# Sigmoid attention and a SiLU layer on one core: bursts of three score tiles instead of two, the third in single PSUM banks

## The chip, the cores and the metric

The kernel runs on one core of one Trainium2 chip. The metric is device time in microseconds (us) of one execution, the median of several runs. Engines are named as in the profile: PE is TensorE's matmul queue, PEld its weight loads, DVE is VectorE, ACT is ScalarE, POOL is GpSimd, SP is SyncE, which here issues transposes and stores.

## The reference

Attention over 8 batches, 12 heads, 448 positions and 64 channels a head, with a sigmoid in place of the softmax, and behind it a dense layer, SiLU, and a second dense layer:

```python
scores = scale * np.matmul(q, k.transpose(0, 1, 3, 2)) - np.log(S)
attn = 1.0 / (1.0 + np.exp(-scores))
x = np.matmul(attn, v)                  # 8 x 12 x 448 x 64
x = x.transpose(0, 2, 1, 3).reshape(3584, 768)
h = x @ w_in                            # 768 -> 2048
g = h * (1.0 / (1.0 + np.exp(-h)))
out = g @ w_out                         # 2048 -> 768
```

Inputs and output are float32; the kernel computes with float16 operands and float32 sums.

## The kernel before

The 12 heads of a batch are worked on in three groups of four, so there are 24 groups (g) in all. A group's keys are cut into seven pieces (ch) of 64 positions. One piece of one group is a unit, or a tile of scores; there are 168, in the order of `units`, 21 to a batch.

**Scores** (`scores`, L168 to L186). Four 64x64 matmuls with 448 columns each fill a PSUM tile `psc` of two banks; they run side by side in the four quarters of TensorE. Then one activation on ACT (L184) reads both banks, takes the sigmoid with scale and with the bias tile `bias_s`, and writes `attnT` in float16. `psc` comes from the pool `ps_sc`, which has two such tiles and so four banks.

**Values** (`values`, L195 to L221). When the seven pieces of a group are there, seven rounds of four 64x64 matmuls add up in two banks `pav`; two DVE instructions (L219) copy them into `xT`.

**The dense layers** are a stream, written as a generator (`all_moe`). `h_unit` (L230 to L252) does one of 16 column blocks of the first layer for one batch: six 128x128 matmuls with 448 columns into a bank `ph`, a sigmoid on ACT (L248, `tsig`), a product on DVE (L249) into `gTr`. The second layer works on sets (`out_set`): a pair of row blocks is computed with seven products of half size in place of eight, each of eight matmuls with 384 columns into a bank `po` (`product`, L307), whose sums and differences DVE makes before (tiles `S1` to `S4`, from `gTr`) and after (L315, some banks with two readers). The first product of a set is copied by ACT (L322, `m`). The third product takes its weights from the first sum, `sg[2]` (tile `S3`), which DVE computes behind the last `gTr` of the batch.

`ph`, `po` and `pav` come from the pool `ps_1`, a ring of four single banks (tag `ps1`). The pool hands out the bank that was released longest ago in the program's order.

**The order** is written out by hand (`manual_schedule`): each engine does its instructions in the order of the program, and a wait holds whatever stands behind it on that engine. The last loop alternates a burst of scores with a piece of the stream. `stretch(ns)` adds ns to what is due, and takes steps of the stream, each with its planned time (189 ns an h matmul, 163 ns one of a product), until that much is done; it can stop inside an h unit or a product. `hold` keeps it going from the last h unit of a batch to the copy of the next set's first product. With each burst, `values_if_any` does the values of a group that is complete, and `rows_if_any` prepares one transpose: a copy on DVE (`kr` or `qr`, L163), a DMA transpose on SP, and behind q's the loads of k and q of a later group on POOL. `after_values` loads v. The piece of the stream behind a burst of two has a length by batch, `paces`, from 2,000 ns in batch 2 to 3,400 ns in batches 4 and 5.

Of the kernel before, what the change touches and what calls it, by code (L numbers as in the profile page):

```python
# [11 lines left out]
F32 = mybir.dt.float32  # L12
AF = mybir.ActivationFunctionType
# [4 lines left out]
def kernel(  # L18
# [9 lines left out]
    nc = tc.nc  # L28

    B, H, S, D = q.shape  # L30
    NT, DMODEL = out.shape
    DFF = moe_w_in.shape[1]
    P = 128
    HP = P // 2
    NCH = S // HP
    NPAIR = H // 2
    NQ = NPAIR // 2
    NT_B = NQ * NCH
# [7 lines left out]
    QKSCALE = 1.0 / math.sqrt(D)  # L46
# [7 lines left out]
    ps_sc = ctx.enter_context(tc.tile_pool(name="ps_sc", bufs=2, space=bass.MemoryType.PSUM))  # L54
    ps_1 = ctx.enter_context(tc.tile_pool(name="ps_1", bufs=4, space=bass.MemoryType.PSUM))
# [45 lines left out]
    bias_s = cpool.tile([P, 1], F32, tag="biass", name="bias_s")  # L101
# [65 lines left out]

    attnT = {}  # L168

    def scores(g, ch):  # L170
        attnT[g, ch] = p12.tile([P, 2, S], F16, tag="attnT", name="attnT")
        psc = ps_sc.tile([P, 2, 512], F32, tag="pssc", name="psc")
        for half in range(2):
            own = slice(half * HP, (half + 1) * HP)
            for j in range(2):
                rows = slice(j * D, (j + 1) * D)
                nc.tensor.matmul(  # L177
                    psc[own, j, :S],
                    qkT["k", g][rows, ch, own],
                    qkT["q", g][rows, :, own],  # L180
                    start=True,
                    stop=True,
                )
        nc.scalar.activation(  # L184
            attnT[g, ch], psc[:, :, :S], AF.Sigmoid, bias=bias_s, scale=QKSCALE
        )  # L186

    xT = {}
    ready = set()
# [4 lines left out]
    def values(g, end=NCH):  # L194
        b, iq = divmod(g, NQ)  # L195
        if b not in xT:
            assert b < 2 or b - 2 in h_done
            xT[b] = p2.tile([P, NPAIR, S], F16, tag="xT", name="xT")
        pav, done_rounds = part_of.pop(g, None) or (
            [ps_1.tile([P, 512], F32, tag="ps1", name="pav") for _ in range(2)],  # L200
            0,
        )
        for ch in range(done_rounds, end):
            at = attnT.pop((g, ch))
            for half in range(2):
                own = slice(half * HP, (half + 1) * HP)
                for j in range(2):
                    nc.tensor.matmul(  # L208
                        pav[half][j * D : (j + 1) * D, :S],
                        flat["v", g][own, j, ch, :],  # L210
                        at[own, j, :],
                        start=(ch == 0),
                        stop=(ch == NCH - 1),
                    )
        if end < NCH:
            part_of[g] = pav, end
            return
        for half in range(2):
            nc.vector.tensor_scalar_mul(xT[b][:, half * NQ + iq, :], pav[half][:, :S], SX)  # L219
        if iq == NQ - 1:  # L220
            ready.add(b)  # L221
# [177 lines left out]
    def stretch(ns):  # L399
        nonlocal done, due  # L400
        due += ns
        while done < due or hold:
            step_ns = next(stream, None)
            if step_ns is None:
                break
            done += step_ns
# [19 lines left out]
    units = [(g, ch) for g in range(NQB) for ch in range(NCH)]  # L426
    waiting = []
# [12 lines left out]
    def after_values(g):  # L440
        if g == 0:
            load("v", 3)
            load_w_in(2)
            load_w_in(3)
        elif g == 1:
            load("v", 4)
            load_w_out(0, 0)
            load_w_out(0, 1)
        elif g == 2:
            load("v", 5)  # L450
            load_w_out(1, 0)
            load_w_out(1, 1)
            load("kq", 6)
            load("kq", 7)
        elif g + 3 < NQB:
            load("v", g + 3)
        if g == 6:
            for to in (10, 11, 12):
                load("kq", to)
        if g == 5:  # L460
            load("kq", 9)
        if g >= 6 and g + 3 < NQB:
            later.extend(((g + 3, "k"), (g + 3, "q")))
# [3 lines left out]
    def rows_if_any():  # L467
        if later:
            g, name = later.pop(0)
            dma_transpose(g, name, nc.vector.tensor_copy)  # L470
            if name == "q" and g + 4 < NQB and g + 4 > 12:
                load("kq", g + 4)

    def values_if_any():
        if waiting:
            g = waiting.pop(0)
            values(g)
            after_values(g)
# [9 lines left out]
    def transposes(g, name):  # L488
        pe_transpose(g, ((name, 0, 4), (name, 4, NCH)))
        if name == "q":  # L490
            after_transpose(g)
# [35 lines left out]
    for n in range(NT_B + 3):  # L527
        scores(*units[n])
        for do, *what in behind.get(n, ()):
            do(*what)  # L530

    paces = {1: 1600, 2: 2000, 3: 2550, 4: 3400, 5: 3400, 6: 3000, 7: 3000}
    stretch(paces[1])
    for n in range(NT_B + 3, len(units), 2):
        burst = units[n : n + 2]
        if n == 2 * NT_B:
            values_if_any()
            stretch(21500)
        for u in burst:
            scores(*u)  # L540
        values_if_any()
        rows_if_any()
        for g, ch in burst:
            if ch == NCH - 1:
                waiting.append(g)
        if n in (24, 30):
            transposes(4 + (n - 24) // 6, "k")
        elif n in (26, 32):
            transposes(4 + (n - 26) // 6, "q")
        stretch(paces[1] if 1 not in ready else paces[n // NT_B])  # L550
    for g in waiting:
        values(g)
    for _ in stream:
# [31 lines left out]
```

## Time and profile before

| | us |
|---|---|
| median of 3 runs (382.05 to 382.88) | 382.63 |
| the profiled execution | 382.75 |
| its span, from the first to the last instruction | 381.0 |
| ACT, sigmoid of a tile of scores, mean of 168 | 1.016 |
| ACT, sigmoid of an h unit, mean of 128 | 0.545 |
| DVE, product of an h unit, mean of 128 | 0.623 |
| DVE, copy out of a values bank, mean of 48 | 0.619 |
| DVE, copy of the rows for a transpose | 0.61 |
| DVE, read of a product's bank | 0.55 |

The profiled execution's time is that of the profile's own run, 1.75 us of it outside the span. In the profile's groups, the number behind the bar is the busy time of the group, then the mean of one instruction in ns, then the idle time of its engine just before. The length of a matmul is that of its way through the array; matmuls overlap, and the distance between the starts of two neighbours is what one costs. In the timeline, instructions of one kind that follow each other are merged into one line with their number behind the x; the first number is the start, the second the time to the end of the last. Where a line says idle, it is the time that the engine waited ahead of it, with what ended the wait. A bank's wait is found in the start of a matmul behind its neighbour.

The granted TensorE clock is 1.00 throughout.

### The profile page before, as it was taken

To read this page: it belongs to the slowest core of one execution; us is meant where nothing else is said; L and a number is where in the kernel's file an instruction comes from. 1 tells how busy PE (TensorE), PEld (TensorE's weight loads), DVE (VectorE), ACT (ScalarE), POOL (GpSimd) and SP (SyncE) were. 2 spreads that over 40 slices of the span, in tenths; PEclk is the share of its full clock that TensorE was granted. 3 is DMA by queue.
4 is the path that set the end of the run, shared out by engine and by line. 5 is a ranking of instruction groups with operands and counts; after the bars stand their busy time and mean duration, and the time that the engine had idled before them with its cause. 6 is when DMAs were issued, how large, how long until landed. Compare 5 with 4: busy or idle time off the path is not lost.

```text
span 381.0 us, 7663 instructions
## 1 busy us (share of the span) xinstructions
PE 372.2 (98%) x3083; PEld 186.9 (49%) x3083; DVE 233.8 (61%) x415; ACT 240.0 (63%) x328; POOL 92.9 (24%) x158
## 2 busy tenths in 40 slices
PE   7999999999999999999999999999999999999995
PEld 2444445545554445444555444544455444555663
DVE  2446646996565666556767547735857446656773
ACT  4998886758777875778444686577774787044000
POOL 8855326202752323121311303101100000000000
PEclk9999999999999999999999999999999999999999
DMA  7999999974999936937939859535346300110233
GB/s 112 180 188 204 205 203 181 155 103 101 166 236 232 141 51 97 184 47 75 152 68 191 96 112 122 56 101 74 48 77 105 83 3 2 41 41 2 75 92 83
DMA packets 66403, 42.71 MB, mean 112 GB/s; under 512 B 37056, under 2 KB 62912, under 8 KB 66368
## 3 DMA queue, kind: packets, MB, share of 16 engines
q0 software_dynamic: 28032, 22.69, 42.7%
q1 hardware_dynamic: 38112, 19.31, 28.2%
q8 instruction: 24, 0.39, 0.4%
q10 hardware_dynamic: 224, 0.23, 0.2%
q14 instruction: 11, 0.09, 0.1%
HBM read 45.61 MB, written 11.01 MB: 149 GB/s over the span
## 4 chain that ended last, share of the span: by engine, by line
PE 80%; DMA 12%; DVE 2%; ACT 2%; POOL 1%; issue 1%; DVEq 0%
PE po L307 34%; PE ph L236 29%; PE psc L177 9%; PE pav L208 6%; DMA w_in_sb<-in_moe_w_in_dram 6%; DMA w_out_sb<-in_moe_w_out_dram 5%; DVE gTr L249 1%; DMA ks<-in_k_dram 1%; ACT attnT L184 1%; DMA vf<-in_v_dram 1%; DVE T L278 1%; POOL qf L78 1%; PE pw L135 1%; POOL kf L78 0%; ACT qr L138 0%
## 5 line engine op out<-in xcount | busy, mean ns | idle before, releaser
L184 ACT ACTIVATE attnT<-psc,bias_s 128x896 f16<-128x896 f32 x168 | 158.9, 1016 | 53.3 <-PE psc L177 53.2
L236 PE MATMUL ph<-xT,w_in_sb 128*128 128x448 f16 x768 | 153.2, 353 | 0.0
L249 DVE TENSOR_TENSOR gTr<-ph,tsig 128x448 f16<-128x448 f32 x128 | 78.1, 623 | 72.0 <-ACT tsig L248 71.4
L236 PEld LDWEIGHTS <-w_in_sb 128*128 128x128 f16 x768 | 71.9, 98 | 75.7 <-issue 12.9
L248 ACT ACTIVATE tsig<-ph 128x448 f16<-128x448 f32 x128 | 68.2, 545 | 47.8 <-PE ph L236 46.2
L78 POOL DMA_DIRECT2D vf<-in_v_dram x48 | 28.7, 613 | 140.7 <-PE pav L208 140.2
L307 PEld LDWEIGHTS <-S 128*128 128x128 f16 x448 | 42.3, 98 | 33.9 <-issue 6.8
L315 DVE SCALAR_TENSOR_TENSOR osb<-po,osb 128x384 f32<-128x384 f32 x70 | 37.7, 555 | 25.1 <-PE po L307 24.5
L177 PE MATMUL psc<-qT,kT 64*64 64x448 f16 x672 | 50.4, 362 | 2.5 <-ACT attnT L184 1.2
L219 DVE TENSOR_SCALAR xT<-pav 128x448 f16<-128x448 f32 x48 | 27.7, 619 | 30.3 <-PE pav L208 30.3
L307 PE MATMUL po<-T,S 128*128 128x384 f16 x224 | 40.6, 327 | 0.1
L307 PEld LDWEIGHTS <-gTr 128*128 128x128 f16 x304 | 28.7, 98 | 23.4 <-issue 5.2
L307 PE MATMUL po<-w_out_sb,S 128*128 128x384 f16 x224 | 39.9, 326 | 0.0
L208 PE MATMUL pav<-attnT,vf 64*64 64x448 f16 x672 | 37.9, 349 | 0.4 <-DVE gTr L249 0.4
L78 POOL DMA_DIRECT2D qf<-in_q_dram x48 | 28.9, 612 | 38.1 <-DVE qr L163 16.9
L307 PE MATMUL po<-w_out_sb,gTr 128*128 128x384 f16 x192 | 34.7, 327 | 0.0
L177 PEld LDWEIGHTS <-kT 64*64 64x64 f16 x672 | 15.0, 104 | 32.8 <-issue 30.9
L78 POOL DMA_DIRECT2D kf<-in_k_dram x48 | 28.9, 612 | 7.0 <-DVE kr L163 4.4
L208 PEld LDWEIGHTS <-vf 64*64 64x64 f16 x672 | 20.2, 107 | 12.4 <-issue 1.9
L315 DVE SCALAR_TENSOR_TENSOR osb<-po,m 128x384 f32<-128x384 f32 x42 | 23.2, 552 | 4.1 <-PE po L307 2.5
L322 ACT ACTIVATE m<-po 128x384 f32<-128x384 f32 x14 | 6.9, 491 | 23.7 <-PE po L307 23.7
L307 PE MATMUL po<-T,gTr 128*128 128x384 f16 x112 | 21.4, 326 | 0.0
(40 smaller groups left out, 131.0 us busy)
## 6 DMA issues: line engine op xcount, KB each, us to landing
out_dram<-osb SPq DMA_DIRECT2D x54, 192.0 KB, 2.9
qf<-in_q_dram POOLq DMA_DIRECT2D x48, 112.0 KB, 5.8
vf<-in_v_dram POOLq DMA_DIRECT2D x48, 112.0 KB, 4.8
kf<-in_k_dram POOLq DMA_DIRECT2D x46, 112.0 KB, 5.5
w_in_sb<-in_moe_w_in_dram POOLq DMA_DIRECT2D x4, 768.0 KB, 10.5
w_out_sb<-in_moe_w_out_dram POOLq DMA_DIRECT2D x4, 768.0 KB, 17.0
kT<-kr SPq DMA_TRANSPOSE x18, 5.6
qT<-qr SPq DMA_TRANSPOSE x18, 6.2
```

The source lines that it names most:

```text
L78: nc.gpsimd.dma_start(flat[name, g][half * HP : (half + 1) * HP, :, c0:c1].rearrange("p i c d -> p i (c d)"), source[name][b, h0 : h0 + 2] ...
L135: nc.tensor.matmul(pw, dummy[:, :P], dummy, start=True, stop=True)
L177: nc.tensor.matmul(psc[own, j, :S], qkT["k", g][rows, ch, own], qkT["q", g][rows, :, own], start=True, stop=True,)
L184: nc.scalar.activation(attnT[g, ch], psc[:, :, :S], AF.Sigmoid, bias=bias_s, scale=QKSCALE)
L208: nc.tensor.matmul(pav[half][j * D : (j + 1) * D, :S], flat["v", g][own, j, ch, :], at[own, j, :], start=(ch == 0), stop=(ch == NCH - 1),)
L219: nc.vector.tensor_scalar_mul(xT[b][:, half * NQ + iq, :], pav[half][:, :S], SX)
L236: nc.tensor.matmul(ph[:, :S], w_in_sb[:, cc, fc * P : (fc + 1) * P], xT[b][:, cc, :], start=(at == 0), stop=(at == NCC - 1),)
L248: nc.scalar.activation(tsig, ph[:, :S], AF.Sigmoid, bias=0.0, scale=ISX)
L249: nc.vector.tensor_mul(gTr[:, fc, (b % 2) * S : (b % 2) * S + S], ph[:, :S], tsig)
L307: nc.tensor.matmul(po[:, :NO2], a[:, fc, :], w[:, fc, :], start=(fc == 0), stop=(fc == NHC - 1))
L315: nc.vector.scalar_tensor_tensor(out=o, in0=po, scalar=sign, in1=x, op0=ALU.mult, op1=ALU.add)
L322: nc.scalar.activation(m1, po, AF.Copy, scale=ISX)
```

## The change

From batch 2 on, without batch 3, a burst has three tiles. It has two where a group waits for its values. The first of the three gets two single banks of the ring `ps_1`, and its sigmoid becomes two activations of 448 elements, one for each bank; the other two use the pool `ps_sc` as before. The piece of the stream behind a burst is as long per tile as before: `ns * tiles / 2`. What follows a burst (values, one transpose, the list of groups that wait) is done as before, once a burst. The part ahead of batch 2 keeps its order.

```diff
-    def scores(g, ch):
+    def scores(g, ch, banks=None):
         attnT[g, ch] = p12.tile([P, 2, S], F16, tag="attnT", name="attnT")
-        psc = ps_sc.tile([P, 2, 512], F32, tag="pssc", name="psc")
+        if banks is None:
+            psc = ps_sc.tile([P, 2, 512], F32, tag="pssc", name="psc")
+            banks = [psc[:, j] for j in range(2)]
+            parts = [(attnT[g, ch], psc[:, :, :S])]
+        else:
+            parts = [(attnT[g, ch][:, j], banks[j][:, :S]) for j in range(2)]
...
-                    psc[own, j, :S],
+                    banks[j][own, :S],
...
-        nc.scalar.activation(
-            attnT[g, ch], psc[:, :, :S], AF.Sigmoid, bias=bias_s, scale=QKSCALE
-        )
+        for to, psc in parts:
+            nc.scalar.activation(to, psc, AF.Sigmoid, bias=bias_s, scale=QKSCALE)
+
+    def single_banks():
+        return [ps_1.tile([P, 512], F32, tag="ps1", name="psc1") for _ in range(2)]
...
+    TILES = {2: 3, 3: 2, 4: 3, 5: 3, 6: 3, 7: 3}
     paces = {1: 1600, 2: 2000, 3: 2550, 4: 3400, 5: 3400, 6: 3000, 7: 3000}
-    stretch(paces[1])
-    for n in range(NT_B + 3, len(units), 2):
-        burst = units[n : n + 2]
-        if n == 2 * NT_B:
-            values_if_any()
-            stretch(21500)
-        for u in burst:
-            scores(*u)
+    def burst(n, tiles):
+
+        new = units[n : n + (tiles if not waiting else 2)]
+        for i, u in enumerate(new):
+            scores(*u, single_banks() if i == len(new) - 3 else None)
         values_if_any()
         rows_if_any()
-        for g, ch in burst:
-            if ch == NCH - 1:
-                waiting.append(g)
+        waiting.extend(g for g, ch in new if ch == NCH - 1)
+        return len(new)
+
+    stretch(paces[1])
+    for n in range(NT_B + 3, 2 * NT_B, 2):
+        burst(n, 2)
...
+    values_if_any()
+    stretch(21500)
+    n = 2 * NT_B
+    while n < len(units):
+        ns = paces[n // NT_B]
+        tiles = burst(n, TILES[n // NT_B])
+        n += tiles
+        stretch(ns * tiles / 2)
```

More of the change, by code (lines that the diff above doesn't have):

```diff
@@ L549 @@
             transposes(4 + (n - 26) // 6, "q")
-        stretch(paces[1] if 1 not in ready else paces[n // NT_B])
+        stretch(paces[1])
+    values_if_any()
[6 more added lines that the diff above has]
+        stretch(ns * tiles / 2)
     for g in waiting:
```

## Prediction

> **What bounds the kernel now.** I read the busy table first, then the waits, then the timeline of TensorE. The busy table:
>
> ```profile
> PE 372.2 (98%) x3083; PEld 186.9 (49%) x3083; DVE 233.8 (61%) x415; ACT 240.0 (63%) x328; POOL 92.9 (24%) x158
> ```
>
> PE works 98% of the span; every other engine has a third or more to spare. The waits of PE, from the view of who waited for whom:
>
> ```profile
> PE pw L135 <- DVE bias_s L422: 1.5, 1, 1.5
> PE psc L177 <- ACT attnT L184: 1.2, 4, 0.5
> PE psc L177 <- DVE qT L155: 0.5, 1, 0.5
> PE pav L208 <- DVE gTr L249: 0.4, 1, 0.4
> ```
>
> In 381 us the matmul queue waits 3.6 us. So what counts is the sum of TensorE's own work, anything that makes it wait is added whole, and neither DMA nor the 37% idle ScalarE can give anything by itself. Now PE's timeline in batch 4:
>
> ```profile
> 169.21 1.11 PE L236 MATMUL ph<-xT,w_in_sb 128*128 128x448 f16 x5
> 170.25 0.57 PE L177 MATMUL psc<-qT,kT 64*64 64x448 f16 x8
> 170.76 3.58 PE L236 MATMUL ph<-xT,w_in_sb 128*128 128x448 f16 x18
> 174.26 0.57 PE L177 MATMUL psc<-qT,kT 64*64 64x448 f16 x8
> ...
> 183.60 0.57 PE L177 MATMUL psc<-qT,kT 64*64 64x448 f16 x8
> ...
> 187.62 0.57 PE L177 MATMUL psc<-qT,kT 64*64 64x448 f16 x8
> ```
>
> Columns are start and length. Eighteen h matmuls and one burst of two tiles take 174.26 - 170.25 = 4.01. In the long run at the end 96 h matmuls take 18.16, 0.189 each, so 3.41 for 18. Tiles of scores inside a block follow at 0.189 (in the values at 209.29 seven rounds of the same 64x64 form take 1.43 to the next product at 210.72). 4.01 - 3.41 - 0.38 leaves 0.22 to 0.23 that a burst costs for going to 64x64 and back. Between products: 187.62 - 183.60 = 4.02, less 21 x 0.162 (runs of 20 and 21 differ by 0.162), less 0.38: 0.24. **A burst has an entry price of 0.23**, whatever its number of tiles.
>
> **The gain.** The order of the instructions is fixed by the program. The 126 tiles of scores of batches 2 to 7 stand in 63 bursts of two before and in 50 bursts after: 26 of three, 24 of two (batch 3, and each burst with values). 13 entries fall away: 13 x 0.233 = **3.03 us** off PE. The tiles themselves stay: 13 fewer bursts move 26 tiles into others, as third tile, at 0.187 to 0.189. The upper bound of a third tile is that of a tile alone, 0.31 (10.95 to 11.26). I take 0.189: it is the same form as the values' rounds, which keep 0.189 through seven rounds although each brings four weight loads. Nothing else that PE issues changes in number.
>
> **ScalarE.** 26 sigmoids of 896 become 52 of 448 that carry the bias tile. No such row exists. The nearest rows:
>
> ```profile
> L184 ACT ACTIVATE attnT<-psc,bias_s 128x896 f16<-128x896 f32 x168 | 158.9, 1016 | 53.3 <-PE psc L177 53.2
> L248 ACT ACTIVATE tsig<-ph 128x448 f16<-128x448 f32 x128 | 68.2, 545 | 47.8 <-PE ph L236 46.2 <-DVE T L278 0.6
> L322 ACT ACTIVATE m<-po 128x384 f32<-128x384 f32 x14 | 6.9, 491 | 23.7 <-PE po L307 23.7
> L138 ACT ACTIVATE kr<-kf 128x896 f16<-128x896 f16 x3 | 2.8, 942 | 0.0
> L423 ACT ACTIVATE warm<-bias_s 128x1 f32<-128x1 f32 x1 | 0.3, 294 | 0.0
> ```
>
> tsig and m differ by 64 elements and 54 ns: 0.84 ns an element, and 0.17 us beside it. attnT has 0.26 beside its 896 elements, though kr of the same length has 0.19. What attnT has and the others lack is a bias tile or the two rows of a bank pair. warm, one element with a bias tile, takes 0.294, so I give the 0.09 to the bias, and each half pays it. Back to back, starts are 0.89 apart after an attnT (four take 3.70) and 0.42 after a tsig (three at 253.93 take 1.49), 0.12 under their lengths. A half then takes 448 x 0.84 + 0.26 = 0.63, and holds the engine 0.51. Bounds: 0.42 (as tsig) and 0.63 (no overlap). Two halves cost 1.03 for 0.89. [...]
>
> ScalarE does not bound: a cycle of 24 h matmuls takes PE 24 x 0.189 + 0.69 + 0.1 = 5.3, ScalarE 1.03 + 2 x 0.89 + 4 x 0.42 = 4.5. But it is a queue, and a tsig behind a burst starts late.
>
> **The ring, which is where the gain goes.** ph, po, pav and now psc1 share four banks; the pool hands out the one released longest ago in program order. A burst of three needs two of them at once, and the second is often that of the last-but-one unit; PE stands in order, so a wait there holds the whole stream. I followed each of the 26 bursts with the intervals above. On VectorE, behind a values block and in h work:
>
> ```profile
> 92.23 1.15 PE L307 MATMUL po<-w_out_sb,gTr 128*128 128x384 f16 x6
> ...
> 92.34 1.16 DVE L219 TENSOR_SCALAR xT<-pav 128x448 f16<-128x448 f32 x2 [0.96 <-PE pav L208]
> 93.41 0.61 DVE L163 COPY kr<-kf 128x896 f16<-128x896 f16 x1
> 93.94 0.55 DVE L315 SCALAR_TENSOR_TENSOR osb<-po,m 128x384 f32<-128x384 f32 x1
> ```
>
> ```profile
> 170.25 0.57 PE L177 MATMUL psc<-qT,kT 64*64 64x448 f16 x8
> ...
> 170.69 1.91 ACT L184 ACTIVATE attnT<-psc,bias_s 128x896 f16<-128x896 f32 x2
> 172.48 1.11 ACT L248 ACTIVATE tsig<-ph 128x448 f16<-128x448 f32 x2
> ...
> 173.06 1.19 DVE L249 TENSOR_TENSOR gTr<-ph,tsig 128x448 f16<-128x448 f32 x2 [1.17 <-ACT tsig L248]
> ```
>
> - (a) After batch 2's second values a burst of three comes 12 product matmuls later, 12 x 0.162 + 0.1 = 2.05. Its second bank is that of the product finished right behind the values. By the first fence the two copies and kr go ahead on VectorE: first reader 1.71 after the products start (93.94 - 92.23), second 0.47 later, 0.56 long, 0.05 to PE: 2.78. **Wait 0.73.**
> - (b) Once, in batch 7, the burst comes 18 matmuls after values (3.03) and needs the next product's bank, whose reader follows the second on the same tile: 2.76 + 0.56 + 0.05 = 3.36. **0.33.**
> - (c) Twice (batches 5 and 7) the burst cuts the last h unit but one at 3 of 6. Scores' sigmoids start 0.44 after the burst (second fence); 1.03 + 1.78 later comes the cut unit's tsig (3.25), the last unit's at 3.67; gTr follows 0.58 behind (3.83, 4.37), then the S sum (0.68, start 4.91): the third product's weights are there at 5.65. PE: 0.69 + 9 x 0.189 + 16 x 0.162 = 4.98. **2 x 0.65.**
> - (d) Twice, in batch 7, the burst cuts a unit at 5 of 6. Its bank comes round to the fourth unit behind: wanted at 0.69 + 0.19 + 3 x 1.136 = 4.29, free at 3.25 + 0.58 + 0.62 + 0.05 = 4.50. **2 x 0.2.** Cut at 3 of 6 it is wanted 0.38 later and does not wait.
> - (e) Four bursts find the second bank 0.03 to 0.2 late behind such a chain: **0.3.**
>
> Sum 3.1. The same bookkeeping of the kernel before puts its two waits in this stretch at 0.65 and 0.27, where the matmul starts in the trace show 0.64 and 0.23; I shave to **2.8**. The wait at 143.8 (batch 3, four sigmoids in a row) stays.
>
> Moved steps: rows and their transposes (SP), k, q and v loads (POOL) go with the bursts; each group still has two bursts or more for its two transposes, and k and q come three groups ahead, so I price that at nothing; if a copy found its load late, VectorE would hold the products at its price.
>
> Sum: -3.03 + 2.8 = **-0.2 us**. The profiled execution took 382.75 (span 381.0 and 1.75 around it), so 382.5; the median of the runs is 0.1 lower: **382.4**. Under 0.2% (0.77 us) a measurement of this kernel can't be told from no change.
>
> **Rivals.**
> - A, chance 0.20: the halves go as tsig does, 0.42. Then (c) is 0.44 each, (d) nothing, (e) 0.15: waits 2.1, -0.93, **381.7**. For it: the plain form; against: warm.
> - B, 0.06: the banks come free in time and the waits stay out: **379.6**. Against: the two waits already there.
> - C, 0.07, slower: neighbours on ScalarE do not overlap in this form, 0.63 a half. The 0.23 falls whole on (c) and (d), part of it on (e), and four bursts lose their margin: waits 4.6, +1.6, **384.2**. It is slower by 0.2% from about 0.58 a half on. Against: each form in this trace overlaps its neighbour by 0.1.
> - D, 0.04, slower: the third tile's weights can't come ahead and it costs 0.31: 26 x 0.125 = 3.2, **385.6**; it decides from 0.23 a tile on. Against: the seven rounds. [...]
> - E, 0.03: fewer bursts save nothing and add no waits, **382.6**.
>
> **How the numbers follow.** The forecast has 0.60, its own range 381.8 to 383.0. The range 381.0 to 383.4 leaves out B, C and D and the ends of the others. Faster by over 0.2%: B, two thirds of A, a tenth of the forecast and more, 0.28. Slower: C, D and a twentieth of the forecast, 0.14. Within: 0.58.
>
> **What would show it.** PE's score blocks of three should take 0.69; the half sigmoids 0.63 long and 0.51 apart; a wait of about 0.7 on the first three-tile burst behind batch 2's second values; two waits of the third product on S. Wrong if the halves are 0.54 long, if waits stand elsewhere, or if scores of three take over 0.75.

## The result and the profile after

The changed kernel takes 383.34 us (median of 16 runs), the kernel before 382.57 in the same rounds: a ratio of 1.0018, 95% interval 1.001 to 1.0026. It is **slower by 0.4 to 1.0 us**, where the prediction had 0.2 us less. The time lies inside the stated range (381.0 to 383.4), the sign is wrong.

The busy table of the profiled execution after (383.69 us, span 381.9):

```profile
PE 370.8 (97%) x3083; PEld 189.6 (50%) x3083; DVE 232.0 (61%) x415; ACT 241.7 (63%) x354; POOL 92.9 (24%) x158
```

PE's busy time fell by 1.4 us, and yet the span grew by 0.9. (Busy time still holds part of each wait: of one of 0.74, shown below, its line counts 0.37. So the fall is less than what the bursts gave.) The waits of PE's matmul queue, after:

```profile
PE pw L135 <- DVE bias_s L430: 1.5, 1, 1.5
PE psc L183 <- ACT attnT L191: 1.2, 4, 0.5
PE psc L183 <- DMA qT<-qr: 0.6, 1, 0.6
PE po L315 <- DVE S L327: 0.5, 2, 0.3
PE ptrk L148 <- DVE kf L432: 0.5, 1, 0.5
PE psc L183 <- DVE qT L155: 0.4, 1, 0.4
PE pav L216 <- DVE gTr L257: 0.4, 1, 0.4
PE ph L244 <- DVE gTr L257: 0.4, 1, 0.4
PE psc L183 <- DVE osb L323: 0.4, 1, 0.4
```

Five of these lines are new. One (`ptrk`) belongs to the first 41 us, whose order did not change. Three are the ring and the S sum that the prediction named; the fifth, q's transpose, it had priced at nothing. PE's timeline after, first a burst of three between products, then the one behind batch 2's second values block:

```profile
187.54 0.76 PE L183 MATMUL psc<-qT,kT 64*64 64x448 f16 x12
188.24 1.15 PE L315 MATMUL po<-w_out_sb,S 128*128 128x384 f16 x6
```

```profile
102.45 0.37 PE L183 MATMUL psc<-qT,kT 64*64 64x448 f16 x1
103.19 0.76 PE L183 MATMUL psc<-qT,kT 64*64 64x448 f16 x11 [0.37 <-DVE osb L323]
103.88 0.34 PE L315 MATMUL po<-w_out_sb,gTr 128*128 128x384 f16 x1
```

From the burst's start to the next product's it is 188.235 - 187.541 = 0.69; a burst of two takes 0.50 to 0.51, so a third tile costs 0.19, as taken. In the second fence one matmul has started, and the next, for the second single bank, starts 103.19 - 102.45 = 0.74 later. The line itself says only 0.37: a wait counts there from the end of the matmul before (102.45 + 0.37 = 102.82). **Starts show the whole of a wait.**

The halves, in the groups of instructions by form:

```profile
L191 ACT ACTIVATE attnT<-psc,bias_s 128x448 f16<-128x448 f32 x52 | 30.1, 630 | 30.4 <-PE psc L183 30.4
```

0.63 each, as worked out from the rows of before.

To compare executions I take the stretch in which the two kernels differ: from the start of the first product's first matmul (76.91 before, 76.38 after) to the start of the first product behind the last h matmul (349.30 before, 350.16 after). The part ahead of it has the same order in both, and its end lies between 76.4 and 77.1 in the profiles here; behind it come products alone.

| execution | that stretch, us | against before |
|---|---|---|
| before | 272.39 | |
| after, first profile | 273.78 | +1.39 |
| after, second profile (the run "again") | 272.97 | +0.58 |

The second profile's +0.58 lies within the interval of the timed runs; the 0.81 more of the first is one event, below.

### The profile page after: what moved, and what is told of

Read it like the earlier page. It is cut to its first block, busy times and chain, and to the rows that moved or that the text cites. A ratio compares the mean times of both kernels' runs of the same rounds, so it can differ in the third digit from the quotient of the medians.

```text
span 381.9 us, 7689 instructions
## 1 busy us (share of the span) xinstructions
PE 370.8 (97%) x3083; PEld 189.6 (50%) x3083; DVE 232.0 (61%) x415; ACT 241.7 (63%) x354; POOL 92.9 (24%) x158
## 4 chain that ended last, share of the span: by engine, by line
PE 78%; ACT 9%; DMA 7%; DVE 4%; issue 2%; ACTq 0%; DVEq 0%
PE ph L244 31%; PE po L315 31%; PE psc L183 8%; ACT attnT L191 7%; PE pav L216 7%; DMA qT<-qr 4%; DVE gTr L257 2%; DMA kT<-kr 2%; DMA ks<-in_k_dram 1%; ACT tsig L256 1%; DVE T L286 1%; DVE S L327 0%; DVE osb L323 0%; PE ptrq L148 0%; PE ptrk L148 0%
## 5 line engine op out<-in xcount | busy, mean ns | idle before, releaser
L191 ACT ACTIVATE attnT<-psc,bias_s 128x896 f16<-128x896 f32 (+1 forms) x194 | 161.4, 916 | 52.6 <-PE psc L183 52.5
L257 DVE TENSOR_TENSOR gTr<-ph,tsig 128x448 f16<-128x448 f32 x128 | 76.8, 620 | 76.7 <-ACT tsig L256 76.5
L256 ACT ACTIVATE tsig<-ph 128x448 f16<-128x448 f32 x128 | 66.5, 549 | 48.4 <-PE ph L244 48.1
L183 PE MATMUL psc<-qT,kT 64*64 64x448 f16 x672 | 49.1, 360 | 3.3 <-ACT attnT L191 1.2
L183 PEld LDWEIGHTS <-kT 64*64 64x64 f16 x672 | 16.9, 104 | 31.9 <-issue 28.7
```

Source lines behind the costliest of these rows:

```text
L183: nc.tensor.matmul(banks[j][own, :S], qkT["k", g][rows, ch, own], qkT["q", g][rows, :, own], start=True, stop=True,)
L191: nc.scalar.activation(to, psc, AF.Sigmoid, bias=bias_s, scale=QKSCALE)
L256: nc.scalar.activation(tsig, ph[:, :S], AF.Sigmoid, bias=0.0, scale=ISX)
L257: nc.vector.tensor_mul(gTr[:, fc, (b % 2) * S : (b % 2) * S + S], ph[:, :S], tsig)
```

## The experiments

**Is what the first profile shows part of the change?** The kernel unchanged, with a second profile.

> The changed kernel once more, for a second profile. In the first profile ten places wait that the prediction had on its list (3.2 us together, without the late start below) and two that it had not: the scores of the first tile of group 11 wait 0.81 us for q's DMA transpose, and one sigmoid starts 0.34 us late (301.85). Theory 1, these are part of the change: both stand here too, within 0.1. Theory 2, they belong to one execution: the DMA wait is away or under 0.2, the late sigmoid gone, and the ten others stand as they were.

Measured: one run, 383.31; PE in the second profile:

```profile
132.85 0.57 PE L183 MATMUL psc<-qT,kT 64*64 64x448 f16 x8
133.35 0.93 PE L244 MATMUL ph<-xT,w_in_sb 128*128 128x448 f16 x4
```

and in the first:

```profile
132.37 0.38 PE L183 MATMUL psc<-qT,kT 64*64 64x448 f16 x4
133.37 0.38 PE L183 MATMUL psc<-qT,kT 64*64 64x448 f16 x4 [0.62 <-DMA qT<-qr]
133.69 0.55 PE L244 MATMUL ph<-xT,w_in_sb 128*128 128x448 f16 x2
```

In the first the second tile starts 1.00 behind the first, in the second the burst takes its 0.50. The wait for q's transpose is not a fixed part of the change: the two q transposes issued between 110 and 136 us landed after 14.8 and 11.5 us there, and after 9.2 and 5.7 in the second profile. The late sigmoid, however, is in both: at 301.5 (second profile) the scores' first sigmoid starts 0.77 behind the burst, where a burst that finds ScalarE and its banks free has 0.43 to 0.44. So neither theory holds for both; the ten waits stood as they were.

**Where does it sit?** The changed kernel, with `TILES` set to three in some batches alone.

```diff
-    TILES = {2: 3, 3: 2, 4: 3, 5: 3, 6: 3, 7: 3}
+    TILES = {2: 3, 3: 2, 4: 2, 5: 2, 6: 2, 7: 2}   # only2
+    TILES = {2: 2, 3: 2, 4: 3, 5: 3, 6: 3, 7: 3}   # only4567
+    TILES = {2: 2, 3: 2, 4: 3, 5: 2, 6: 3, 7: 2}   # only46
```

> Bursts of three in batch 2 alone; the order up to 143 us is that of the changed kernel. 3 bursts fewer, 3 x 0.233 = 0.70 saved; the ring wait behind the second values block costs 0.73. Theory 1 (the transposes come too late through the change to batch 2): another 0.8 for the q of group 11, so +0.8 against the kernel before. Theory 2 (that wait is chance): 0.0, within 0.2.

> Bursts of three in batches 4 to 7, batch 2 as before. 10 bursts fewer, 2.33 saved. Theory 1, ring waits only: 0.65 twice, 0.2 to 0.56 and 0.2, 0.4, 0.24 and small ones, 2.4 to 2.8, so +0.1 to +0.5, and no DMA wait. Theory 2 (the loss of 0.77 sits in these batches, since batch 2 comes out even): +0.75.

> Bursts of three in batches 4 and 6 alone, where the list has waits of 0.05 and 0.07 only. 5 bursts fewer: -1.17 + 0.1 = -1.05 against the kernel before. Rival, a burst of three has a price of its own in each place (12 such bursts of the 26): above -0.7; rival, fewer bursts save nothing: 0.0.

| kernel | bursts fewer | ratio to before, interval | stretch against before, us |
|---|---|---|---|
| only2 | 3 | 1.0012 (0.9991 to 1.0032) | +0.01 |
| only4567 | 10 | 1.0006 (0.9997 to 1.0015) | +0.27 |
| only46 | 5 | 0.997 (0.996 to 0.998) | -1.02 |

only2 comes out even in its trace (3 x 0.233 against 0.71 of waiting) and shows no wait for a transpose; its interval is too wide to say so by time. only46 is the clean one: it gains 1.0 us, where 1.05 was expected, so a burst saved is worth its 0.233, and a burst of three has no hidden price of its own. The loss is nearly all in certain places of batches 2, 5 and 7 (0.24 of it is in batch 6). only2 and only4567 together are +0.28, and the changed kernel has +0.58; the 0.3 between them is the late sigmoid: in only4567 the h unit behind that burst waits 0.29, in the second profile of the changed kernel 0.57.

**What is the late sigmoid?** Six activations of one element more, where ScalarE is idle (1.23 us from 57.19 on in the first profile).

```diff
     values_if_any()
+    for _ in range(6):
+        nc.scalar.activation(warm, bias_s, AF.Sigmoid, bias=bias_s, scale=1.0)
     stretch(21500)
```

> The changed kernel with six more activations of one element on ScalarE at 57 us, where it is idle, so that each later instruction of ScalarE has a number higher by six. It tells apart why one sigmoid started 0.33 late at 302 us in both profiles. Theory, it belongs to the number of the instruction in ScalarE's own stream: the burst at 302 starts its sigmoids 0.43 to 0.44 behind, its wait falls from 0.56 to 0.2, -0.3 against the changed kernel. Rival, it belongs to that burst: the late start stands, no difference.

The burst at 302 us, in the second profile of the changed kernel:

```profile
301.53 0.76 PE L183 MATMUL psc<-qT,kT 64*64 64x448 f16 x12
302.22 3.77 PE L244 MATMUL ph<-xT,w_in_sb 128*128 128x448 f16 x19
302.30 2.96 ACT L191 ACTIVATE attnT<-psc,bias_s 128x448 f16<-128x448 f32 x4 [1.06 <-PE psc L183]
...
306.40 1.11 PE L244 MATMUL ph<-xT,w_in_sb 128*128 128x448 f16 x5 [0.41 <-DVE gTr L257]
```

and with six more:

```profile
302.03 0.76 PE L183 MATMUL psc<-qT,kT 64*64 64x448 f16 x12
302.51 2.96 ACT L191 ACTIVATE attnT<-psc,bias_s 128x448 f16<-128x448 f32 x4 [0.78 <-PE psc L183]
...
302.72 5.00 PE L244 MATMUL ph<-xT,w_in_sb 128*128 128x448 f16 x24
```

The sigmoid's distance from its burst falls from 302.30 - 301.53 = 0.77 to 0.48, and the stretch of 24 h matmuls behind it gets shorter by 0.28; the unit's wait falls from 0.57 to 0.29. In the trace a pause of 0.325 stands behind the 447th instruction of ScalarE's queue (semaphore and DMA instructions counted) in both profiles of the changed kernel, and with six more it stands behind the 447th again, now at 297.5, where nobody waits. So the theory held: it belongs to the place in the stream. What happens there the profile does not show. The time as a whole did not fall (1.0011, 0.9998 to 1.0025): this profile has a wait of 0.3 for a q transpose at 80 us instead.

**Which wait is it in the places behind a cut h unit?** The first S sum is made three h units earlier.

```diff
     def moe_h(b):
         for fc in range(NFC):
+            if fc == NFC - 3 and b > 1:
+                sums_of[b] = first_sum(2 if b % 2 else 0)
...
-        nc.vector.tensor_sub(sg[2], a1[:, lo], a2[:, lo])
+        if early_sum is None:
+            nc.vector.tensor_sub(sg[2], a1[:, lo], a2[:, lo])
```

> The changed kernel, with the first S sum of a set (the operand of its third product) made on VectorE three h units ahead of the batch's end in place of behind the last gTr. Theory: in the two places where a burst cuts the last h unit but one, the third product's wait (0.44 of the 0.65 to 0.67) goes and the second product's wait for the last gTr (0.18) stays, so 0.9 less than the changed kernel: -0.3 to -0.1 against the kernel before. Rival, the third product waits for its bank: no difference from the changed kernel, +0.6 to +0.8.

Changed kernel, second profile, then with the sum first:

```profile
235.04 2.99 PE L315 MATMUL po<-w_out_sb,gTr 128*128 128x384 f16 x16
238.29 0.99 PE L315 MATMUL po<-T,S 128*128 128x384 f16 x5 [0.26 <-DVE S L327]
239.21 0.57 PE L183 MATMUL psc<-qT,kT 64*64 64x448 f16 x8
```

```profile
235.66 2.99 PE L325 MATMUL po<-w_out_sb,gTr 128*128 128x384 f16 x16
238.49 0.98 PE L325 MATMUL po<-T,S 128*128 128x384 f16 x5
239.39 0.57 PE L183 MATMUL psc<-qT,kT 64*64 64x448 f16 x8
```

The third product starts 2.83 behind the first in place of 3.25, and the other place gives as much: the wait was the S sum. The ratio to before is 1.0004 (0.9982 to 1.0026), its medians 382.44 and 382.68. The stretch is +0.34; without a load that came late in that one execution it would be -0.29, as expected. (A load of k landed at 102.61 in place of 101.84, the copy into kr behind it started at 102.69 in place of 102.08 and held the products' reads, and the burst at 103 us waited 0.63 more.)

**Is the price of a half that of the bias?** The halves take no bias tile; they leave out the term -ln S for the tiles in single banks.

```diff
         for to, psc in parts:
-            nc.scalar.activation(to, psc, AF.Sigmoid, bias=bias_s, scale=QKSCALE)
+            bias = bias_s if len(parts) == 1 else 0.0
+            nc.scalar.activation(to, psc, AF.Sigmoid, bias=bias, scale=QKSCALE)
```

> The changed kernel, with the two half sigmoids of a burst's first tile without the bias tile; they leave out the term -ln S for these tiles. Theory, the 0.09 us that a sigmoid of scores has beyond its elements belongs to the bias tile: the halves fall from 0.63 to 0.54, their starts from 0.52-0.53 apart to 0.42-0.44, and by the ring's bookkeeping the places behind ScalarE shorten as rival A of the prediction said: third and second product 0.44 together in place of 0.67 twice, the fourth unit's bank 0.2 less twice. Together 0.8 to 1.0 less than the changed kernel, -0.1 to -0.4 against the kernel before. Rival, the 0.09 belongs to scores as such (their type, place or scale): 0.63 stays, no difference.

```profile
L192 ACT ACTIVATE attnT<-psc 128x448 f16<-128x448 f32 x52 | 25.4, 541 | 31.1 <-PE psc L183 31.1
```

0.541 in place of 0.630: the 0.09 is the bias tile's. The starts of two halves lie 0.42 to 0.44 apart. The stretch falls by 0.97 against the changed kernel's second profile (272.00 us), 0.39 under the kernel before; by time it can't be told from the kernel before (1.0001, 0.999 to 1.0013). This is rival A's mechanism, on the waits that A named: behind the cut units 0.47 in place of 0.66 for each third product, 0.38 and 0.03 in place of 0.57 and 0.22 in (d). Its price of -0.93 was not reached, above all because 0.41 of (d) stays, which A put at nothing and most of which is the late sigmoid, described above.

**Does the order of the banks decide, or how early they are asked for?**

```diff
-            scores(*u, single_banks() if i == len(new) - 3 else None)
+            scores(*u, single_banks() if i == 2 else None)
```

> The changed kernel, with the third tile of a burst, not the first, in the two single banks. PE asks for the two banks 0.4 later, but their sigmoids stand behind the pair tiles' and free them 1.8 later, and the next units take just these banks. Theory, the waits are those of the ring worked out burst by burst: the waits at the burst's own second bank go, new ones of 0.3 to 0.85 come behind 14 bursts, +3.0 against the kernel before (2.5 to 3.5). Rival, what matters is how early the burst asks for its banks: the waits behind values and in front of the burst (1.4) go and none come, -0.8.

Measured 1.0108 (1.0088 to 1.0128), +4.2 in the stretch. The rival is out: bursts ask for their banks later, and what follows waits. The waits are larger than worked out, and the sum lies beyond the 2.5 to 3.5 expected: the largest was put at 0.85, and two h units wait 1.24 and 0.89. Behind the burst at 303 us PE's line shows who holds the bank:

```profile
303.43 0.76 PE L183 MATMUL psc<-qT,kT 64*64 64x448 f16 x12
304.13 1.50 PE L244 MATMUL ph<-xT,w_in_sb 128*128 128x448 f16 x7
...
304.22 2.96 ACT L191 ACTIVATE attnT<-psc,bias_s 128x896 f16<-128x896 f32 x4 [1.08 <-PE psc L183]
306.70 1.11 PE L244 MATMUL ph<-xT,w_in_sb 128*128 128x448 f16 x5 [1.08 <-ACT attnT L191]
```

Here, too, the first sigmoid starts 0.79 behind its burst: the late start again, on the worst spot.

**Three tiles where nobody waits.** Two tiles in the seven places with a wait.

```diff
-        new = units[n : n + (tiles if not waiting else 2)]
+        two = n in (58, 123, 139, 149, 157, 160, 165)
+        new = units[n : n + (tiles if not waiting and not two else 2)]
```

> Bursts of three from batch 2 on, with two tiles in the seven places where the list of waits has one (and, as groups come out, in batch 3 and behind values as before): 24 bursts of three, 51 bursts in place of 63. 12 x 0.233 = 2.8 saved, waits of 0.18, 0.07, 0.05 and 0.18 left, and the wait of 0.64 in batch 3 goes, since the first product is cut in another place: -2.9 against the kernel before (-2.4 to -3.3). Rival, a burst of three has a price of its own wherever it stands: above -2.0.

Measured 380.03, **0.9927** (0.9909 to 0.9945), -2.76 in the stretch. PE's waits in it:

```profile
PE pw L135 <- DVE bias_s L430: 1.5, 1, 1.5
PE psc L183 <- ACT attnT L191: 0.8, 3, 0.4
PE psc L183 <- DVE qT L155: 0.5, 1, 0.5
PE pav L216 <- DVE gTr L257: 0.4, 1, 0.4
```

None of the new lines is left; by the starts two h units still wait 0.29 and 0.23 for their bank, too short for a line. With 24 bursts of three it beats both kernels; the changed kernel has 26. Not all of the gain is that of the bursts, though. The kernel before has this wait in batch 3:

```profile
143.78 0.38 PE L177 MATMUL psc<-qT,kT 64*64 64x448 f16 x4
144.64 0.38 PE L177 MATMUL psc<-qT,kT 64*64 64x448 f16 x4 [0.48 <-ACT attnT L184]
```

The second tile starts 144.64 - 143.78 = 0.86 behind the first, where it is 0.21 without a wait. That is a wait of 0.65, and the changed kernel has it too. In chosen_places the stream stands elsewhere there, the two bursts lie 3.04 apart in place of 1.59, and the wait is gone (three waits for `attnT` in place of four). So the sum is -2.80 for 12 bursts, -0.65 for batch 3, and +0.59 for the waits that are left: -2.86, measured -2.76. Without the wait of batch 3, which has nothing to do with a third tile, it would be about -2.1: that much the bursts could give all the time, and a handful of places gave it back.

## Why the prediction was wrong

- **The gain, 3.03: right.** 13 bursts fewer, 0.69 for a burst of three, and only46's 1.02 for 5 bursts. From the waits below, 3.58 - 0.58 = 3.00.
- **The half sigmoid: right**, 0.63 by sum and by measurement, and by the cause given.
- **The places of the waits: right** for (a) to (d), and four bursts wait as in (e), 0.02 to 0.24, though (e) names no places (its row below has a wait of 0.04 in an h unit besides). No other of 0.1 or more is new in both profiles.
- **The size of the ring's term, 2.8: this step failed; it measured 3.58.** By the starts of the second profile:

| | predicted | measured |
|---|---|---|
| (a) behind batch 2's second values | 0.73 | 0.71 |
| (b) 18 matmuls behind values | 0.33 | 0.40 |
| (c) third product, twice | 1.30 | 1.31 |
| (d) unit cut at 5 of 6, twice | 0.4 | 0.57 + 0.22 |
| (e) small ones | 0.3 | 0.37 |
| sum | 3.1, taken as 2.8 | 3.58 |

Two things turned the sign. The first is the shave from 3.1 to 2.8: two waits of the kernel before, off by 0.01 and 0.04, were made into a tenth of everything. Without it the sum was +0.07. The second is in (d): the cut unit's bank had a margin of -0.2, so a late start on ScalarE goes into PE, and one of the two bursts had its sigmoid 0.34 late. Where it was not late (only4567, six_more) the same unit waited 0.29 in place of 0.57. So 0.3 from the first and 0.28 from the late sigmoid are most of the 0.78 between 2.8 and 3.58; the rest is a tenth more in (d) and some hundredths in (b) and (e). The 0.65 of (c) is a slip, for its own 5.65 - 4.98 is 0.67, but the runs show 0.66. The pause on ScalarE was in no row that the prediction read.

- **Moved steps at nothing: open, and not safe.** The range had no term for it. Of the six profiles with 26 bursts of three, three have a wait of TensorE for a load or a transpose in the stretch, each in another place (0.80 in the first, 0.31 in six_more, 0.63 in sumfirst); the five others, the kernel before and chosen_places among them, have none. That points at the change, but single executions don't show it. The timed runs' +0.77 is 0.2 more than the second profile's +0.58, and such waits may be that 0.2; so may the one profile of the kernel before, whose run lay 0.18 above that kernel's median. No run here separates the two.
- **Rivals.** A was refuted by the row (0.63); no_bias shows its mechanism, with -0.39 in the stretch and not -0.93. B fell with the waits. C would have needed halves that do not overlap; the starts of two halves lie 0.52 to 0.53 apart. D fell with 0.69 a burst; E with only46. The outcome on the slower side came not from a rival but from the forecast's own case, with a few tenths more in its waits; its own range ended at 383.0, 0.4 above the median it stood on, and the measured +0.77 is beyond that. As gain and loss were both 3 us, the difference hung on a tenth of either. That it would end near zero was foreseen; -0.2 as the likeliest did not follow from its own sum of 3.1. The prediction also held that under 0.2% a change can't be told from none: the 16 runs of each kernel tell 0.18%, with an interval from 0.10% to 0.26%.

## What to carry to other kernels

When a stage is bound by one engine that works in the program's order (PE here, 97 to 98% busy), an edit that saves switches there (0.23 us each here) and borrows buffers from a ring should be judged place by place: work out for each place who releases the bank that comes round, and leave the edit out where that is late. Add the waits as worked out, without a discount from two samples. On a queue that is 85% full (4.5 of 5.3 us here, worked out from the rows), one sigmoid that started 0.29 later (0.77 behind its burst, 0.48 in six_more) cost the stream 0.28, so a margin of a few tenths is no margin there.

## What the runs showed of the hardware that was not expected

- ScalarE paused for 0.325 us behind the 447th instruction of its queue in this program (302.29 to 302.61 in the first profile), in both profiles of the changed kernel and with six instructions added ahead of it; nothing in the profile ends the pause.
- A half sigmoid (128x448 out of PSUM) took 0.630 us with the bias tile and 0.541 without it, 0.09 less. The prediction had this from one row of a single element; no_bias shows it.
- One and the same q transpose landed after 14.8 us in one execution and after 9.2 in another of the same order, the next one after 11.5 and 5.7.
